# Turning six more tiles by DMA, and moving the output product of turned tiles behind the MLP block

## The chip, the core and the metric

The kernel runs on one core of a Trainium2 chip. The core has TensorE (PE in the profile; its weight loads are PEld), VectorE (DVE), ScalarE (ACT), GpSimd (POOL) and SyncE (SP), which issues nearly all DMAs. Each engine works through its own queue in the order in which the program names the instructions; they meet only in semaphores. The metric is the device time of one execution in microseconds (us), lower is better.

## What is computed

A pre-norm transformer layer on 2048 tokens of 512 channels, in float32: dilated local attention (32 heads of 16 channels, a window of 8 positions at distance 2), then an MLP of 1792 hidden channels with a squared relu.

```python
qkv = layernorm(x) @ wqkv                        # q, k, v: 32 heads x 16
idx = pos[:, None] - 2 * arange(8)[None, :]      # positions before 0 are masked
attn = softmax(einsum("bhsd,bhswd->bhsw", q, k[idx]) * 16 ** -0.5)
o = einsum("bhsw,bhswd->bhsd", attn, v[idx])
h = x + o @ wo
r = relu(layernorm(h) @ w1 + b1)
out = h + (r * r) @ w2 + b2
```

## The kernel before

**Tiles.** The 2048 tokens are 16 tiles of 128, t = 0 to 15, in four groups of four (R = 4): tiles 0 to 3 are group 0. Within a group a tile has a place i = t % 4; RI = 2 divides the places into a first and a second pair.

**Products.** Every float32 product is made of three products of numbers that are split into a high and a low part (`hi` on ACT, `lo` on DVE or POOL): high x high, and the two of high x low. That is `mm3`, 12 matmuls a block. With `lows_last` the four matmuls that need the low part of the left operand come last of the twelve. A left operand must lie turned (transposed). PE does that in four matmuls with the identity (`transposes`); the result is in PSUM, ACT casts the high part and DVE subtracts for the low part.

**Turned by DMA.** Tiles in `OV` have their attention result o, and tiles in `HV` their normalised h, turned without PE: `turn_split` (ACT, line 594) takes the float32 words apart into two planes of 16 bits, `turn_dma` (SP, line 598) turns these with a transposing DMA, and `turn_join` (ACT, line 603) puts the words together. Then follow the high part (ACT) and the low part (`lo_T`; DVE in the kernel before). Both sets are (4, 5, 8, 9, 12, 13) before: the first pair of groups 1 to 3. In this text a turned tile is one that is turned by DMA.

**Stages.** First x is normalised and multiplied with `wqkv` (`qkv`, `qkv_of`), tiles 0 to 3 by head groups and then two tiles at a time (`first_phase`, t0 = 4, 6, ... 14). The slots there are half products (6 matmuls). For group 0 a counter k runs over them: k = 0 to 11 lies in the call for t0 = 12, k = 12 to 23 in that for t0 = 14, and negative k in that for t0 = 10. The attention of the tiles runs beside it, chiefly on DVE (dots, weights, sums) and POOL (`add_up`, line 411). At set k group 0 gets its output product (`WO` = 7, 9, 13, 15 for tiles 0 to 3) and h is turned. A turning of o by PE stands at `OT`; `OK` and `HK` give the k of split, DMA and join for tiles turned by DMA.

Then come four MLP passes, u = 0 to 3, one for each group. A slot p of passes 0 to 2 holds one block of the first MLP product (`mlp1`, 12 matmuls), and one of the second (`mlp2`, 12 matmuls), which lags by LAG = 3 slots. In pass u, the next group u + 1 is prepared: its o is turned at slots `OP`, its output product is made at slots `WP` = 9, 10, 13, 14, its h is turned at 15 and 16. So tile 4 has its output product in slot 9 of pass 0 and tile 5 in slot 10.

**Order of the work.** There are two lists of chores for each slot: `due` (entered by `at`) and `late` (entered by `after`). At the end of a slot `end_slot` runs the due list, then `pump`, then the late list. `pump` puts attention operations into the queues as long as the planned DVE time `now["dve"]` is below the planned PE time `now["pe"]`; `pump(until=s)` goes on until the attention of the tile pair s is in the queues. As engines do not leave their order, a chore's place in these lists sets what it waits behind.

**Around the output product.** `wo_product` enters `h_add` (DVE adds the product to h, then the statistics of h), `h_norm`, `add_b2` and `spill` for the slots to come. For tiles in `AS` the statistics are made by ACT (`act_stats`, lines 181 to 183), for the others by DVE (`norm_stats`). In passes 0 to 2 the blocks of `mlp1` and of `wo_product` take the PSUM banks mm0 and mm1 in turn (`Turn.tile`). A bank of `mlp1` is read by `hidden` (ACT: relu, line 846), which `mlp1` enters in the due list of the next slot. In `first_phase` four banks are taken in turn.

Of the kernel before, what the change touches and what calls it, by code (L numbers as in the profile page):

```python
# [19 lines left out]
R = 4  # L20
# [8 lines left out]
NEG = -4.0e9  # L29
ROWS = 15  # L30
LAG = 3
AS = (4, 5, 8, 9, 12, 13)
OV = (4, 5, 8, 9, 12, 13)
HV = (4, 5, 8, 9, 12, 13)
SLOW = 1.01, 1.10, 1.06
DELAY = 3
WJ = 2
# [1 line left out]
OT = 4, 5, 10, 12  # L39
WO = 7, 9, 13, 15  # L40
HT = 20, 20, 21, 23
OK = (-6, -2, 4), (-5, -1, 5), (3, 6, 10), (4, 7, 12)
HK = (12, 15, 18), (14, 16, 19)
W2 = (18,)
LH = 3, 4, 10, 11
OP = 6, 7, 12, 13
# [12 lines left out]
def block_kernel(ctx, tc, x, wqkv, wo, w1, b1, w2, b2, out):  # L59
# [154 lines left out]
        for d, src in parts(tr, h_dst):  # L214
            hi(d, src)

    def lo_T(tr, h_dst, l_dst):
        for (d, src), h in zip(parts(tr, l_dst), h_dst):
            lo(nc.vector, d, src, h)
            dve(0.16 + 0.53 / len(h_dst))  # L220

    def mm3(ps, lh, ll, rh, rl, mid=None, at_=2 * KB, lows_last=False):

# [388 lines left out]
    def o_join(t):  # L612
        turn_join(("o", t))
        tr = planes.pop(("o", t))
        if t % R == RI:
            ohl = att.tile([P, 2, KB, P], F32R, name="ohl", tag="o", bufs=3)
            oT[t] = ohl[:, 0], ohl[:, 1]
        else:
            oT[t] = row("oh", (P, KB, P), F32R), row("ol", (P, KB, P), F32R)
        hi_T(tr, [oT[t][0]])  # L620
        after(0, lo_T, tr, [oT[t][0]], [oT[t][1]])

    def h_split(t):
        turn_split(("h", t), hn.pop(t))
# [33 lines left out]
    def wo_product(t, slots):  # L658
        ps = turn["mm"].tile("wo")
        oh, ol = oT.pop(t)  # L660
        mm3(ps, lambda k: oh[:, k, :], lambda k: ol[:, k, :],
            lambda k: wo_h[:, k, :], lambda k: wo_l[:, k, :], lows_last=t in OV)
        for n, (fn, a) in zip(slots, ((h_add, (t, ps)), (h_norm, (t,)), (add_b2, (t,)),
                                      (spill, (t,)))):
            (after if fn in (h_norm, spill) else at)(n + (fn is add_b2), fn, *a)

# [311 lines left out]
    def first_phase(t0):  # L980
        def chores(m):
            if t0 + 3 < 16:
                if m in (0, 2):
                    at(0, x_stats, t0 + 2 + m // 2)

                early = t0 == 12
                if m + early in (6, 7):
                    at(0, x_norm, t0 - 4 + m + early)
                if m in XT[early]:
                    x_T(t0 + 2 + XT[early].index(m))  # L990
            if t0 + 5 < 16 and m in (6, 9):
                at(0, load_x, t0 + 2 + m // 3)
            if jobs and m % 3 == 0:
                at(0, weight_job)
            k = t0 // 2 * 12 - 72 + m
            if k == 19:
                dve(HOLD)
            for t in range(R):
                if k == OT[t]:
                    at(0, load_h, t)  # L1000
                    if t not in OV:
                        o_T(t)
                if t in OV and k in OK[t]:
                    at(0, (o_split, lambda t: turn_dma(("o", t)), o_join)[OK[t].index(k)], t)
                if t in HV and k in HK[t]:
                    at(0, (h_split, lambda t: turn_dma(("h", t)),
                           lambda t: turn_join(("h", t)))[HK[t].index(k)], t)
                if k == WO[t]:
                    wo_product(t, (1, 3, 4, 6))
                    now["pe"] += 2.73  # L1010
                if k == HT[t]:
                    (at(0, h_parts, t) if t in HV else h_T(t))
            if k in W2:
                at(0, load_w2, W2.index(k))

        def half(m):
            end_slot(1.37)
            chores(m)

        for n in range(6):  # L1020
            chores(2 * n)
            qkv_of(t0 + n % 2, n // 2, lambda: half(2 * n + 1))
            end_slot(1.37)
# [41 lines left out]
    for u in range(R - 1):  # L1065
# [11 lines left out]
        for i in js:  # L1077
            t = R * (u + 1) + i
            if not end:
                a = i // 2 if u == 2 else 0  # L1080
                o0 = OP[i] - a
                if t in OV:
                    turned = [(o0, at, 0, o_split, t), (o0, after, 0, turn_dma, ("o", t)),
                              (o0 + 2, at, 0, o_join, t)]
# [26 lines left out]
        for p in range(FB + LAG):  # L1111
            more = 0.0
            if p == FB:
                run(due)
                dve(HOLD)
            if u < 2 and p == FB - 2:
                dve(HOLD)
            for fn, *a in sorted(todo.get(p, []), key=lambda x: x[0] is wo_product):
                fn(*a)
                more += 2.73 if fn is wo_product else 0.0  # L1120
            if p < FB:
                mlp1(u, fs[p])
                more += 2.73
                if first:
                    at(0, split_w2, p)
                    if p + 1 < FB:
                        load_w2(p + 1)
            q = p - LAG
            if q >= 0:
                f = fs[q]  # L1130
                mlp2(u, f, acc, js, q == 0, q == FB - 1,
                     (lambda: half(p)) if p in halves else None)
                more += 2.74
                if f < 12 and (need or first and p < FB - LAG):
                    free.append(place.pop(f))
                    if need:
                        at(1, fetch, need.pop(0))
            end_slot(more)
# [85 lines left out]
```

## Time and profile before

| | |
|---|---|
| median of 3 runs | 512.38 us (511.91 to 513.16) |
| the profiled execution | 512.31 us |
| its span in the profile | 510.5 us |
| granted TensorE clock, mean | 0.999 |
| busy: PE, DVE, ACT, POOL | 501.9, 376.7, 290.9, 351.2 us |
| instructions | 7598 |

The span is what the profiler recorded of the core; the execution's own time has some 1.8 us around it. A row of the time line has the start in us from the span's start, the length in us, the engine, the line of the code, the operation, what it writes and reads, and how many such were merged; in square brackets stands how long the engine was idle before it and what it waited for. In rows of tiles three figures parted by slashes are the lowest, median and highest length in ns. Line numbers can be those of helpers: line 232 is any `mm3`, 870 is `mlp2`, 150 any low part, 147 any high part, 205 a turning on PE, 639 `h_add`.

### The profile page before, as it was taken

What the parts mean: (1) busy time and instruction counts of PE and PEld (TensorE: products, weight loads), DVE (VectorE), ACT (ScalarE), POOL (GpSimd) and SP (SyncE); (2) the same over time, 40 slices, a digit from 0 to 9 for tenths busy, and PEclk for the clock granted to TensorE, in tenths of its full rate; (3) what the DMA queues carried; (4) which work ended last, traced back from release to release, by engine and by line L of the source; (5) the groups of instructions that cost most, each with busy time, mean ns of one, the idle gap of its engine ahead of it and who ended that gap; (6) DMA issues with size and microseconds to landing.
All of it is one profiled execution on the core that took longest, in us unless ns stands there. A gap on an engine that the chain in (4) does not pass through costs nothing. (4 is left out here: it accounts for less than half of the span.)

```text
span 510.5 us, 7598 instructions
## 1 busy us (share of the span) xinstructions
PE 501.9 (98%) x2460; PEld 424.4 (83%) x2460; DVE 376.7 (74%) x512; ACT 290.9 (57%) x552; POOL 351.2 (69%) x430
## 2 busy tenths in 40 slices
PE   7999999999999999999999999999999999999997
PEld 6999788888888888888888878888888888998986
DVE  5479899988998899788879979899963046832233
ACT  4634686767434767485364557264564737666541
POOL 4714799895786798786778768776897364685610
PEclk9999999999999999999999999999999999999999
DMA  8678998989677889666587955767672172444112
GB/s 264 180 225 203 256 295 299 271 285 274 204 225 214 276 301 272 200 199 174 182 253 217 226 166 163 202 199 249 207 152 67 52 217 84 160 142 133 62 42 83
DMA packets 100912, 100.52 MB, mean 197 GB/s; under 512 B 21000, under 2 KB 69384, under 8 KB 100872
## 3 DMA queue, kind: packets, MB, share of 16 engines
q1 hardware_dynamic: 99928, 99.52, 65.4%
q10 hardware_dynamic: 944, 0.52, 0.3%
q8 instruction: 19, 0.31, 0.3%
q14 instruction: 21, 0.17, 0.1%
HBM read 72.65 MB, written 24.25 MB: 190 GB/s over the span
## 5 line engine op out<-in xcount | busy, mean ns | idle before, releaser
L411 POOL TENSOR_TENSOR pr<-pr 128x512 f32<-128x512 f32 (+1 forms) x128 | 132.5, 1035 | 45.7 <-DVE pr L354 40.3
L232 PE MATMUL mm<-big_l,w_h 128*128 128x512 f32 x336 | 88.7, 390 | 0.0
L354 DVE TENSOR_TENSOR pr<-ex,v 128x1024 f32<-128x1024 f32 x64 | 78.2, 1222 | 12.8 <-POOL o L411 6.5
L343 DVE TENSOR_TENSOR pr<-qp,k 128x1024 f32<-128x1024 f32 x64 | 76.9, 1202 | 5.6 <-ACT qp L272 5.5
L377 DVE TENSOR_REDUCE ex<-pr 128x64 f32<-128x1024 f32 x64 | 78.4, 1226 | 1.9
L232 PEld LDWEIGHTS mm<-big_l,w_h 128*128 128x128 f32 x336 | 62.8, 188 | 13.0
L150 POOL TENSOR_TENSOR rl<-r,rh 128x512 fp32r<-128x512 f32 x42 | 56.2, 1339 | 19.6 <-ACT rh L147 16.5
L232 PE MATMUL mm<-big_h,xl 128*128 128x512 f32 (+1 forms) x208 | 56.0, 379 | 0.2 <-DVE xl L150 0.2
L232 PE MATMUL mm<-big_h,xh 128*128 128x512 f32 (+1 forms) x208 | 53.5, 378 | 0.7 <-ACT xh L147 0.7
L232 PE MATMUL mm<-big_l,xh 128*128 128x512 f32 (+1 forms) x208 | 52.8, 375 | 0.0
L870 PE MATMUL acc<-big_l,rh 128*128 128x512 f32 x190 | 52.2, 390 | 0.0
L870 PE MATMUL acc<-big_h,rh 128*128 128x512 f32 x190 | 52.1, 391 | 0.0
L501 ACT COPY y<-mm 128x512 f32<-128x512 f32 (+1 forms) x52 | 28.6, 552 | 41.2 <-PE mm L232 33.0
L870 PE MATMUL acc<-big_h,rl 128*128 128x512 f32 x190 | 51.7, 389 | 0.0
L846 ACT ACTIVATE r<-mm,b_sb 128x512 f32<-128x512 f32 x42 | 28.8, 685 | 32.4 <-PE mm L232 32.3
L232 PE MATMUL mm<-big_l,w_l 128*128 128x512 f32 x168 | 45.0, 389 | 0.0
L232 PEld LDWEIGHTS mm<-big_h,xh 128*128 128x128 f32 x208 | 37.6, 188 | 7.0 <-ACT xh L147 1.5
L232 PEld LDWEIGHTS mm<-big_l,xh 128*128 128x128 f32 x208 | 38.2, 188 | 6.1 <-POOL big_l L150 0.2
L232 PEld LDWEIGHTS mm<-big_h,xl 128*128 128x128 f32 x208 | 37.2, 188 | 5.8 <-DVE xl L150 0.6
L870 PEld LDWEIGHTS acc<-big_h,rl 128*128 128x128 f32 x190 | 35.7, 188 | 7.5
L870 PEld LDWEIGHTS acc<-big_l,rh 128*128 128x128 f32 x190 | 35.5, 188 | 7.4
L870 PEld LDWEIGHTS acc<-big_h,rh 128*128 128x128 f32 x190 | 34.9, 188 | 6.7
(160 smaller groups left out, 904.1 us busy)
## 6 DMA issues: line engine op xcount, KB each, us to landing
k<-qkv_d SPq DMA_DIRECT2D x48, 288.0 KB, 2.8
v<-qkv_d SPq DMA_DIRECT2D x48, 288.0 KB, 3.2
qkv_d<-y SPq DMA_DIRECT2D x18, 512.0 KB, 4.2
big_l<-w2l_d SPq DMA_DIRECT2D x24, 256.0 KB, 3.0
xt<-in_A_x_dram SPq DMA_DIRECT2D x16, 256.0 KB, 4.6
q<-qkv_d SPq DMA_DIRECT2D x32, 128.0 KB, 4.7
h<-in_A_x_dram SPq DMA_DIRECT2D x16, 256.0 KB, 3.9
h_d<-h SPq DMA_DIRECT2D x16, 256.0 KB, 3.2
```

Source lines behind the costliest of these rows:

```text
L150: eng.tensor_tensor(out=dst, in0=src, in1=h, op=ALU.subtract)
L232: nc.tensor.matmul(ps, l(k), r(k), start=(n == 0), stop=(n == 3 * KB - 1))
L343: nc.vector.tensor_tensor(out=pr.rearrange("p i w h d -> p i w (h d)"), in0=qps["now"][:, j % 2].unsqueeze(2).to_broadcast([P, RI, W, GC]) ...
L354: nc.vector.tensor_tensor(out=p2, in1=vwin, op=ALU.mult, in0=e1[:, :, :, j * GH:(j + 1) * GH].unsqueeze(4).to_broadcast([P, RI, W, GH, DH]))
L377: nc.vector.tensor_reduce(out=lf[:, :, :, j * GH:(j + 1) * GH], in_=pr, axis=X, op=ALU.add)
L411: nc.gpsimd.tensor_tensor(out=dst, in0=p2[:, :, :w], in1=p2[:, :, w:2 * w], op=ALU.add)
L501: nc.scalar.copy(y[:, :, t % RI * GC:(t % RI + 1) * GC], ps[:, :j * GC].rearrange("p (j c) -> p j c", j=j))
L846: nc.scalar.activation(r, ps, AF.Relu, bias=b1_sb[:, f:f + 1])
L870: nc.tensor.matmul(acc[j], l[:, j * P:(j + 1) * P], w[f], start=(first and n < len(js)), stop=(last and n >= len(terms) - len(js)))
```

## The change

It has three parts.

1. Group 0 joins: `OV` gets tiles 0 to 3, `HV` and `AS` get tiles 0 and 1. So six blocks (o of four tiles, h of two) are no longer turned by PE but by split, DMA and join. The statistics of h of tiles 0 and 1 go from DVE to ACT. The DMA no longer has a slot of its own: it is entered in the late list of the split's slot, and `OK` and `HK` have two numbers a tile, split and join. Tile 0's o is split at k = -6 and joined at k = 3, tile 1's at -5 and 4, tile 2's at 3 and 10, tile 3's at 4 and 11; h of tile 0 at 11 and 18, of tile 1 at 13 and 19.
2. In passes 0 to 2 the output product of a tile in `OV` (tiles 4, 5, 8, 9, 12, 13) is given to PE behind the slot's `mlp1` block instead of ahead of it, and `h_add` of these tiles goes from the due list of that slot to its late list.
3. The low part of a joined o tile (`lo_T` in `o_join`) is made by GpSimd instead of DVE, and is not counted in `now["dve"]`.

A shift of two slots for tiles of a second pair in `OV` is written too, but no such tile from group 1 on is in `OV`, so it does nothing here.

```diff
-AS = (4, 5, 8, 9, 12, 13)
-OV = (4, 5, 8, 9, 12, 13)
-HV = (4, 5, 8, 9, 12, 13)
+AS = (0, 1, 4, 5, 8, 9, 12, 13)
+OV = (0, 1, 2, 3, 4, 5, 8, 9, 12, 13)
+HV = (0, 1, 4, 5, 8, 9, 12, 13)
...
-OK = (-6, -2, 4), (-5, -1, 5), (3, 6, 10), (4, 7, 12)
-HK = (12, 15, 18), (14, 16, 19)
+OK = (-6, 3), (-5, 4), (3, 10), (4, 11)
+HK = (11, 18), (13, 19)
...
-    def lo_T(tr, h_dst, l_dst):
+    def lo_T(tr, h_dst, l_dst, eng=nc.vector):
         for (d, src), h in zip(parts(tr, l_dst), h_dst):
-            lo(nc.vector, d, src, h)
-            dve(0.16 + 0.53 / len(h_dst))
+            lo(eng, d, src, h)
+            if eng is nc.vector:
+                dve(0.16 + 0.53 / len(h_dst))
...
-        after(0, lo_T, tr, [oT[t][0]], [oT[t][1]])
+        after(0, lo_T, tr, [oT[t][0]], [oT[t][1]], nc.gpsimd if t in (0, 1, 2, 3, 4, 5, 8, 9, 12, 13) else nc.vector)
...
-            (after if fn in (h_norm, spill) else at)(n + (fn is add_b2), fn, *a)
+            late_ = fn in (h_norm, spill) or fn is h_add and t in OV and R <= t and t % R < RI
+            (after if late_ else at)(n + (fn is add_b2), fn, *a)
...
                 if t in OV and k in OK[t]:
-                    at(0, (o_split, lambda t: turn_dma(("o", t)), o_join)[OK[t].index(k)], t)
+                    if k == OK[t][0]:
+                        at(0, o_split, t)
+                        after(0, turn_dma, ("o", t))
+                    else:
+                        at(0, o_join, t)
...
-                o0 = OP[i] - a
+                o0 = OP[i] - a - (2 if i >= RI and t in OV else 0)
...
-            for fn, *a in sorted(todo.get(p, []), key=lambda x: x[0] is wo_product):
+            body = todo.get(p, [])
+            behind = [x for x in body if x[0] is wo_product and x[1] in OV]
+            for fn, *a in sorted(body, key=lambda x: x[0] is wo_product):
+                if [fn, *a] in behind:
+                    continue
                 fn(*a)
                 more += 2.73 if fn is wo_product else 0.0
             if p < FB:
...
+            for fn, *a in behind:
+                fn(*a)
+                more += 2.73
             q = p - LAG
```

The `HK` chores are rewritten in the same way as those of `OK`.

More of the change, by code (lines that the diff above doesn't have):

```diff
@@ L1003, in chores @@
                 if t in OV and k in OK[t]:
-                    at(0, (o_split, lambda t: turn_dma(("o", t)), o_join)[OK[t].index(k)], t)
-                if t in HV and k in HK[t]:
-                    at(0, (h_split, lambda t: turn_dma(("h", t)),
-                           lambda t: turn_join(("h", t)))[HK[t].index(k)], t)
+                    if k == OK[t][0]:
[3 more added lines that the diff above has]
+                        at(0, o_join, t)
+                if t in HV and k in HK[t]:
+                    if k == HK[t][0]:
+                        at(0, h_split, t)
+                        after(0, turn_dma, ("h", t))
+                    else:
+                        at(0, turn_join, ("h", t))
                 if k == WO[t]:
```

## The prediction

> **What bounds the kernel now.** I read the page's busy times first, then the chain of work that ended last, then the waits, and then the time line engine by engine at the three places that the change touches.
>
> ```profile
> PE 501.9 (98%) x2460; PEld 424.4 (83%) x2460; DVE 376.7 (74%) x512; ACT 290.9 (57%) x552; POOL 351.2 (69%) x430
> ```
>
> TensorE (PE) is busy for 98% of the span. So PE work that goes away is a gain, other engines' work counts only where PE waits for it, and little idle time is left to win.
>
> ```profile
> 317.01 0.44 PE tr L205 x4
> 317.45 2.75 PE mm L232 x12
> 320.19 2.72 PE acc L870 x12
> ```
>
> The chain (start, length, what) is PE block after PE block: 12 matmuls of a product take 2.72 us, so four take 0.91; turning a tile on PE takes 0.44 us, and the block behind it 0.03 more: 0.47 a tile.
>
> ```profile
> 294.18 1.07 PE L232 MATMUL wo<-wo_l,oh 128*128 128x512 f32 x4
> 295.86 1.20 PE L232 MATMUL wo<-wo_h,ol 128*128 128x512 f32 x4 [0.61 <-DVE ol L150]
> 296.89 1.08 PE L232 MATMUL mm<-big_l,w_h 128*128 128x512 f32 x4
> ```
> ```profile
> PE wo L232 <- DVE ol L150: 1.2, 2, 0.6
> ```
>
> Here PE waits for VectorE (DVE) inside the output product of tile 8. These eight matmuls should take 1.81 us and take 2.71 (294.18 to 296.89): 0.90 lost, 0.12 of it as slower matmuls after the restart. The waits (total, times, longest) show two such places, tiles 8 and 9: 1.8 us together.
>
> **What the change removes.** Six turnings on PE (o of tiles 0 to 3, h of tiles 0 and 1): 6 x 0.47 = 2.8 us, all on the path. The two waits for the low part: it now comes from GpSimd (POOL), and is wanted one MLP block (2.72 us) later, so they should go: 1.8 us. Gain: 4.6 us.
>
> **What the move behind the MLP block adds.** Look at pass 0, slot 9, where tile 4 has its output product.
>
> ```profile
> 206.83 1.07 PE L232 MATMUL mm<-big_l,w_h 128*128 128x512 f32 x4
> ```
> ```profile
> 203.65 0.68 DVE L150 TENSOR_TENSOR big_l<-raw,big_h 128x512 fp32r<-128x512 f32 x1
> 207.03 0.69 DVE L639 TENSOR_TENSOR h<-wo,h 128x512 f32<-128x512 f32 x1 [2.70 <-PE wo L232]
> 207.64 1.22 DVE L377 TENSOR_REDUCE ex<-pr 128x64 f32<-128x1024 f32 x1
> 208.77 1.22 DVE L343 TENSOR_TENSOR pr<-qp,k 128x1024 f32<-128x1024 f32 x1
> ```
> ```profile
> 207.76 0.63 ACT L181 ACTIVATE scrap<-h 128x512 f32<-128x512 f32 x1 [2.38 <-DVE h L639]
> ...
> 209.47 0.60 ACT L147 CAST big_h<-raw 128x512 fp32r<-128x512 f32 x1
> 209.98 0.68 ACT L846 ACTIVATE r<-mm,b_sb 128x512 f32<-128x512 f32 x1
> ```
>
> Before, the order on PE is product of tile 4, first MLP product of slot 9 (from 206.83), second MLP product (209.55), product of tile 5 (212.27), first MLP product of slot 10 (214.99). DVE adds the product to h from 207.03, 0.20 after the next block began; ScalarE (ACT) takes the statistics of h from 207.76 to 209.47 (1.71 us), and the relu of slot 9 follows in its queue.
>
> PSUM has two banks for these products, taken in turn. With one output product between them, the first MLP products of slots 9 and 10 have the same bank, before and after; slot 10's must wait for slot 9's relu. Before, that relu had time until 214.99. After, PE runs: first MLP product of slot 9, tile 4's product, second MLP product, and then slot 10's first MLP product at once. And the relu still stands behind the statistics of tile 4 in ACT's queue, because h_add moves into the late list of slot 9 and the relu is in the due list of slot 10. Counted from the start of the second MLP product: addition starts at 0.20, statistics 0.73 later, relu 1.71 after that, 0.68 long, some 0.05 to wake PE: 3.4 us. PE is there after 2.72. So PE stalls 0.66, plus 0.12 for the restart: 0.8 us even if DVE is early. The same holds for slot 11 behind slot 10. Six tiles (4, 5, 8, 9, 12, 13): 6 x 0.8 = 4.8 us, which alone eats the gain.
>
> That is the floor; it grows where DVE comes late to the addition. In the late list it stands behind the attention operations that the pump puts into the slot. Pass 0: DVE is free of slot 8's work at about 203.7; five or six operations at some 1.2 us bring it to 209.6 to 210.8, while the product, now from 206.83 to 209.55, lets it start at 209.75. That adds 0 to 1.0; I take 0.5. In slot 10 PE has just lost time and DVE is early. Pass 1 is worse:
>
> ```profile
> 293.69 1.22 DVE L343 TENSOR_TENSOR pr<-qp,k 128x1024 f32<-128x1024 f32 x1
> 294.82 0.97 DVE L150 TENSOR_TENSOR ol<-pl,oh 128x512 fp32r<-128x512 f32 x1
> ...
> 301.68 1.22 DVE L354 TENSOR_TENSOR pr<-ex,v 128x1024 f32<-128x1024 f32 x1 [0.39 <-POOL o L411]
> 302.94 1.23 DVE L377 TENSOR_REDUCE ex<-pr 128x64 f32<-128x1024 f32 x1
> ```
> ```profile
> 292.60 2.11 POOL L411 TENSOR_TENSOR pr<-pr 128x512 f32<-128x512 f32 x2 [1.24 <-DVE pr L354]
> 294.79 0.46 POOL L411 TENSOR_TENSOR o<-pr 128x128 f32<-128x128 f32 x1
> 295.21 1.74 POOL L150 TENSOR_TENSOR rl<-r,rh 128x512 fp32r<-128x512 f32 x1
> ```
> ```profile
> L150 POOL TENSOR_TENSOR rl<-r,rh 128x512 fp32r<-128x512 f32 x42 | 56.2, 1339 | 19.6 <-ACT rh L147 16.5
> ```
>
> Slot 9's PE work starts at 293.27 (294.18 less 0.91) and DVE is still in slot 8 until 294.8. From there the pump puts five operations before the old addition of tile 9, and by its account one more in the new order, with the addition and the low part no longer counted ahead. Run straight through, six operations end at 302.0. But 301.68 shows an operation waiting for POOL's sum of the one before. POOL is free at 295.25; the low part of tile 8, 1.34 us, now comes first, then rl, 1.3, then the sum, 2.65 (292.60 to 295.25): 300.5, and three operations behind it make 304.1. So the addition starts at 302.0 to 304.1, the relu lets PE go 3.2 us later, at 305.2 to 307.3, and PE stands there from 301.43. The stall is 3.8 to 5.9, which is 3.1 to 5.2 above the floor; I take 4.1. Pass 2 has nearly no attention left, and DVE waits long for the product:
>
> ```profile
> 395.11 0.69 DVE L639 TENSOR_TENSOR h<-wo,h 128x512 f32<-128x512 f32 x1 [6.54 <-PE wo L232]
> ```
>
> so it stays at the floor. [...]
>
> **What group 0 adds.** Each tile turned by DMA costs ACT a split, a join and a cast:
>
> ```profile
> L594 ACT COPY pl<-o x6: 1037/1040/1042, 187.2 to 372.5; 128x1024 uint16<-128x1024 uint16 x6
> ...
> L603 ACT COPY pl<-o x6: 1160/1170/1175, 198.1 to 383.8; 128x1024 uint16<-128x1024 uint16 x6
> L147 ACT CAST oh<-pl x6: 621/622/623, 199.3 to 385.0; 128x512 fp32r<-128x512 f32 x6
> L150 DVE TENSOR_TENSOR ol<-pl,oh x6: 683/812/1017, 203.0 to 387.6; 128x512 fp32r<-128x512 f32 x6
> ```
> ```profile
> 120.67 0.59 ACT L501 COPY y<-mm 128x512 f32<-128x512 f32 x1 [0.16 <-PE mm L232]
> 121.16 0.58 ACT L147 CAST oh<-tr 128x512 fp32r<-128x512 f32 x1
> 121.64 0.38 ACT L400 ACTIVATE ex<-ex 128x256 f32<-128x256 f32 x1
> 121.95 0.55 ACT L147 CAST w_h<-raw 128x448 fp32r<-128x448 f32 x1
> 122.40 0.82 ACT L200 ACTIVATE xt<-xt,rs 128x512 f32<-128x512 f32 x1
> ```
> ```profile
> 125.50 0.60 PE L205 MATMUL tr<-ident,xt 128*128 128x128 f32 x4
> ```
>
> At half-slots k=3 and k=4 stand both joins of tiles 0 and 1 and both splits of tiles 2 and 3: each half-slot gets 1.17 + 0.62 + 1.04 = 2.83 us of ACT, against 1.36 of PE. Behind them, at k=5, ACT normalises x tile 14, which PE turns at k=7. ACT is free at 120.51; 2.83, the y copy to its successor 0.49, 2.83, then ex 0.31, w_h 0.45 and xt 0.82 end at 128.2. PE, without two turnings, comes at 125.50 - 0.94 = 124.6: a stall of 3.6 us; some overlap of neighbours makes it 3.5. Low end 2.0, if ACT gets there over a microsecond early; high end 5.0: SyncE (SP) queues each transposing DMA right behind its split, so that the loads of k, q, v, x and weights behind it wait for ACT too. The splits at k=-6 and -5 I cost at nothing (ACT idles in between and has caught up by k=0), the h splits and joins of tiles 0 and 1 too (slots with ACT waiting for PE); without that cover they cost what is in the high end. ACT's new statistics of tiles 0 and 1 replace DVE's and lie behind the products.
>
> **Sum.** 512.3 (the profiled execution's own time, 0.1 below the median of the runs) - 2.8 - 1.8 + 4.8 + 0.5 + 4.1 + 3.5 = 520.6 us. With the ends of its terms: 517.6 to 524.
>
> **Rivals.** A, faster: the floor isn't there. It decides at the start of slot 10's first MLP product: if that block does not have the bank of slot 9, PE never waits for the relu, the move is pure cover, and with the joins covered too the time is 512.3 - 4.6 = 507.7. Against it: the banks alternate strictly, with one product between. For it: nothing in the trace shows a bank; 0.08. B, no change: the floor alone, DVE no longer late in pass 1 and ACT in time at k=5: 512.5. For it: DVE is spared low parts, and its waits for output products go; 0.12. C, slower by less: one of these two large terms comes and not the other, 516 to 517; 0.2. D, slower by more: PE's clock drops after the two long stalls. The start of the kernel has a row:
>
> ```profile
> 1.34 4.18 PE L918 MATMUL tr<-ident 128*128 128x128 f32 x24 [1.34 <-POOL mhalf L904]
> ```
>
> These 24 took 4.18 us, four of them 0.70, against 0.44 later. That is up to 2.0 us per cold start: 520.6 + 4 = 524.6. Against it: no stall before was long enough to show it in mid-run; 0.12. [...]
>
> **How the numbers follow.** The forecast has 0.48, A 0.08, B 0.12, C 0.2, D 0.12. A difference under 0.3% (1.5 us) can't be told from none. Faster is A, 0.08; within 0.3% is most of B, 0.11; slower is the rest, 0.81. The range leaves out A and most of B and goes up past D: 513.4 to 526.
>
> **What would show it.** In the new profile: turnings of o and h down by 24 matmuls; PE idle before the first MLP products of slots 10 and 11 in each pass, released by ACT's relu (line of `hidden`), smallest 0.7, largest in pass 1; PE idle before the turning of x tile 14 near 125, released by ACT. If PE's waits for ACT add up to less than 3 us, I am wrong, and A or B holds.

## The result, and the profile after

The changed kernel takes 537.74 us (median of 4 runs, 537.19 to 539.02) against 512.58 us for the kernel before: ratio 1.0495, 95% interval 1.0472 to 1.0518. It is slower by 25 us. The prediction was 520.6, with a range up to 526.0: the direction was right, the size was not.

The busy times on the page after, and its row of the granted TensorE clock (tenths of full speed, 40 equal slices of the span):

```profile
PE 509.2 (95%) x2436; PEld 426.7 (79%) x2436; DVE 369.1 (69%) x498; ACT 305.8 (57%) x574; POOL 362.0 (67%) x440
PEclk9999999997999999989999997999999999999999
```

The 24 matmuls of six turnings are gone (2460 to 2436), and yet PE is busy 7.3 us longer. The span grew by 26.7 us (510.5 to 537.2). So 19.4 us are more idle time of PE, and 7.3 are matmuls that ran longer, net of the turnings that are gone; the two sevens and the eight in the clock row show where.

The waits of PE after (what it waits for; total us, times, longest):

```profile
PE mm L233 <- ACT r L848: 9.8, 6, 4.3
PE tr L205 <- ACT xt L200: 7.0, 2, 6.6
PE wo L233 <- ACT ohl L147: 1.6, 1, 1.6
PE mm L233 <- ACT y L502: 1.2, 1, 1.2
PE mm L233 <- DVE big_l L150: 0.9, 2, 0.7
```

Before, the largest line behind the start of the kernel was 1.2 us, the wait for the low part. That line is gone. In its place PE waits for ACT: for the relu (line 848, `hidden`), for the normalised x, for a high part, for a copy of y.

The same waits in the time line of PE:

```profile
131.22 1.12 PE L205 MATMUL tr<-ident,xt 128*128 128x128 f32 x4 [6.56 <-ACT xt L200]
228.24 2.07 PE L233 MATMUL mm<-big_l,w_h 128*128 128x512 f32 x4 [4.27 <-ACT r L848]
324.38 2.07 PE L233 MATMUL mm<-big_l,w_h 128*128 128x512 f32 x4 [3.68 <-ACT r L848]
336.00 1.20 PE L233 MATMUL mm<-big_l,w_h 128*128 128x512 f32 x4 [0.48 <-ACT r L848]
```

They are x tile 14; slot 10 of pass 0; slots 10 and 11 of pass 1. Behind each of the three long waits four matmuls take 2.07 us instead of 1.07, or a turning 1.12 instead of 0.66. Three stretches of the table by windows, each right behind one of these waits, have the granted clock at half (the column after POOL's):

```profile
131.20:133.00 1.80, 1.78 (x7) 1.59 (x8) 1.80 (x4) 1.15 (x2) 0.51 (x1) 0.50 1.06 333
...
228.20:230.00 1.80, 1.76 (x4) 1.47 (x5) 1.71 (x4) 1.75 (x4) 1.21 (x4) 0.50 0.81 298
...
324.30:326.30 2.00, 1.92 (x5) 1.54 (x6) 1.88 (x4) 1.93 (x5) 1.32 (x3) 0.50 0.80 251
```

Following the same place of PE's work through both traces (start before, start after, in us) shows where the time goes:

| block | before | after | behind by |
|---|---|---|---|
| first phase, k = 0 | 115.01 | 114.96 | -0.1 |
| first MLP product of pass 0 | 163.29 | 173.40 | 10.1 |
| pass 0, slot 9 | 204.11 | 215.57 | 11.5 |
| pass 0, slot 11 | 220.43 | 238.58 | 18.2 |
| pass 1, slot 9 | 293.27 | 312.38 | 19.1 |
| pass 1, slot 11 | 311.40 | 336.00 | 24.6 |
| pass 3, begin | 432.20 | 459.00 | 26.8 |

Group 0 costs 10.1, the output products of pass 0 cost 6.7, those of pass 1 5.5; the other 4.5 are short waits elsewhere. In the 10.1 are: turnings -2.9, the wait for x tile 14 with its restart 6.7, slow matmuls behind it 2.1, the wait for the high part of tile 2's o 1.9, and two waits for copies of y, 0.8 and 1.6.

### The profile page after: what moved, and what is told of

Read it like the earlier page. It is cut to its first block, busy times and chain, and to the rows that moved or that the text cites. A ratio compares the mean times of both kernels' runs of the same rounds, so it can differ in the third digit from the quotient of the medians.

```text
span 537.2 us, 7582 instructions
## 1 busy us (share of the span) xinstructions
PE 509.2 (95%) x2436; PEld 426.7 (79%) x2436; DVE 369.1 (69%) x498; ACT 305.8 (57%) x574; POOL 362.0 (67%) x440
## 5 line engine op out<-in xcount | busy, mean ns | idle before, releaser
L233 PE MATMUL mm<-big_l,w_h 128*128 128x512 f32 x336 | 92.6, 402 | 12.0 <-ACT r L848 9.8
L355 DVE TENSOR_TENSOR pr<-ex,v 128x1024 f32<-128x1024 f32 x64 | 78.0, 1221 | 10.4 <-POOL o L412 5.2
L150 POOL TENSOR_TENSOR rl<-r,rh 128x512 fp32r<-128x512 f32 x42 | 54.4, 1296 | 17.9 <-ACT rh L147 16.2
L233 PE MATMUL mm<-big_l,w_l 128*128 128x512 f32 x168 | 46.4, 399 | 0.0
L502 ACT COPY y<-mm 128x512 f32<-128x512 f32 (+1 forms) x52 | 28.5, 551 | 20.9 <-PE mm L233 10.4
```

The costliest lines, as they stand in the source:

```text
L150: eng.tensor_tensor(out=dst, in0=src, in1=h, op=ALU.subtract)
L233: nc.tensor.matmul(ps, l(k), r(k), start=(n == 0), stop=(n == 3 * KB - 1))
L355: nc.vector.tensor_tensor(out=p2, in1=vwin, op=ALU.mult, in0=e1[:, :, :, j * GH:(j + 1) * GH].unsqueeze(4).to_broadcast([P, RI, W, GH, DH]))
L502: nc.scalar.copy(y[:, :, t % RI * GC:(t % RI + 1) * GC], ps[:, :j * GC].rearrange("p (j c) -> p j c", j=j))
```

## Experiments

All times are medians. The kernel before, timed along with them, took 511.94 us beside the first four kernels (labels e1 to e4), and 512.43, 511.98 and 512.33 us beside the next three groups of four. "Old sets" means that group 0 is turned by PE, as before.

**One part of the change at a time.** Old sets, all else as changed:

```diff
-AS = (0, 1, 4, 5, 8, 9, 12, 13)
-OV = (0, 1, 2, 3, 4, 5, 8, 9, 12, 13)
-HV = (0, 1, 4, 5, 8, 9, 12, 13)
+AS = (4, 5, 8, 9, 12, 13)
+OV = (4, 5, 8, 9, 12, 13)
+HV = (4, 5, 8, 9, 12, 13)
```

> The changed kernel with group 0 as before (the three sets without tiles 0 to 3); the move behind the MLP block and the low parts on GpSimd stay. Theory 1: the loss has two separate seats, group 0 (10.1 us up to the first MLP pass, 1.3 us just behind it) and the blocks of slots 9 to 11 (13.6 us net in three passes). Then this run is at 537.7 - 11.4 = 526.3 us and keeps PE's waits for ACT's relu in slots 10 and 11. Rival: the second seat is only an after-effect of the first (engines still behind from group 0); then it comes to 514 us or less.

Measured: 522.37, ratio 1.0201 (1.0177 to 1.0226). Parts 2 and 3 alone cost 10.4 us. PE waits for the relu 1.15 and 1.36 us in pass 0, 3.62 in pass 1 (with the slow clock behind it), and 0.47 at three other places. So the second seat stands by itself, as theory 1 has it, but it is 4 us smaller than expected.

Part 1 alone (low parts of group 0 on GpSimd, of the others on DVE; products and `h_add` where they were before):

```diff
-            behind = [x for x in body if x[0] is wo_product and x[1] in OV]
+            behind = []
-            late_ = fn in (h_norm, spill) or fn is h_add and t in OV and R <= t and t % R < RI
+            late_ = fn in (h_norm, spill)
```

> The kernel before with only the first part of the change: tiles 0 to 3 turned by DMA (their low parts on GpSimd, statistics of h of tiles 0 and 1 on ACT); no product moved, low parts of the other tiles on DVE. Theory 1: 512.6 + 11.4 = 524 us, with PE's wait of some 6.6 us before the turning of x tile 14 and the drop of the granted clock behind it. Together with the run that puts group 0 back the two losses add up to that of the whole change (25 us). Rival: the parts cost only together; then this one lies at 512 to 515 us.

Measured: 525.22, ratio 1.0259 (1.0233 to 1.0285), so 13.3 us for a part that was predicted to cost 0.7. The two prices add to 23.7 of the 25 us.

**The late list.** The changed kernel with `h_add` back in the due list (the second edit above alone):

> The changed kernel with h_add of tiles 4, 5, 8, 9, 12, 13 again in the due list, ahead of the pump; the product stays behind the MLP block. Theory 1: the wait for the relu stays, since statistics still stand ahead of it in ACT's queue, but comes down to its floor of 0.64 idle in all six places, and the two drops of the clock go: 537.7 - 5.2 - 5.9 = 526.6 us. Rival: GpSimd's extra low parts make DVE late, not the place of the addition; then the two long stalls of 4.3 and 3.7 us stay and the time is within 2 us of 537.7.

Measured: 546.94, ratio 1.0683 (1.0651 to 1.0714): 9 us worse than the changed kernel, not better. This expectation fell. The time lines of ACT, POOL and DVE of this kernel show what replaced the old wait:

```profile
246.14 0.81 ACT L200 ACTIVATE hn<-h,rs 128x512 f32<-128x512 f32 x1 [6.41 <-POOL rs L190]
246.86 0.67 ACT L848 ACTIVATE r<-mm,b_sb 128x512 f32<-128x512 f32 x1
```
```profile
241.05 2.11 POOL L412 TENSOR_TENSOR pr<-pr 128x512 f32<-128x512 f32 x2 [6.50 <-DVE pr L355]
...
245.91 0.19 POOL L190 TENSOR_TENSOR rs<-nm,rs 128x1 f32<-128x1 f32 x1
```
```profile
233.41 0.69 DVE L640 TENSOR_TENSOR h<-wo,h 128x512 f32<-128x512 f32 x1 [3.65 <-PE wo L233]
```

In the due list the addition waits for the later product (3.65 us) with all of the slot's attention behind it on DVE. POOL's attention sum then waits 6.50 us for DVE; the small operations that finish the statistics stand behind that sum; ACT's normalising waits 6.41 us for them; and the relu stands behind the normalising. PE waited 3.77 us there. In these rows each engine kept the order of its queue, and each stood behind an operation that waited for the next engine.

**Statistics behind the relu.** The changed kernel, with ACT's statistics of tiles 4, 5, 8, 9, 12, 13 entered one slot later, behind the relu:

```diff
-        (act_stats if t in AS else norm_stats)(t, h)
+        if t in AS and t >= R:
+            at(1, stats_norm, t)      # act_stats, then h_norm in the late list
+        else:
+            (act_stats if t in AS else norm_stats)(t, h)
```

> The changed kernel, but ACT's statistics of h of tiles 4, 5, 8, 9, 12, 13 are entered in the due list of the next slot, so that they stand behind the relu of the slot that has the product; h_norm follows them. Product behind the MLP block and late addition as in the change. Theory 1: no wait for the relu is left in slots 10 and 11 (6.7 us in pass 0, 7.4 in pass 1, 1.5 in pass 2, with the drops of the clock): 537.7 - 15.6 = 522 us. Rival: the relu is late because ACT as a whole or DVE is late; then the stalls stay in part and the gain is under 5 us.

Measured: 535.66, ratio 1.0462 (1.0435 to 1.0489), 2 us better than the changed kernel: within the rival's 5, and far from the theory's 522. In pass 0 slot 10's wait went and came back a slot later: PE waited 4.80 us at 242.82, since the normalising that waits for POOL's finish now stood ahead of the next relu (ACT idle 5.07 us there). In pass 1 the wait of 3.68 us gave way to two of 1.19 and 2.48. Moving one chore past one relu handed most of the wait to the next.

**The move and GpSimd's low parts, apart.** Part 2 alone (old sets, low parts on DVE), then part 3 alone (old sets, product and addition as before, by the two edits shown for part 1 alone); for part 2 alone:

```diff
-... nc.gpsimd if t in (0, 1, 2, 3, 4, 5, 8, 9, 12, 13) else nc.vector)
+... nc.vector)
```

> The kernel before with part 2 alone: the products of turned tiles behind the MLP block and their h_add in the late list; group 0 as before, low parts on DVE. It splits the 10.4 us that groups 1 to 3 cost when parts 2 and 3 are there together (522.4 against 511.9). Theory M (the move carries it: the relu of the next slot stands in ACT's queue behind statistics that wait for the later product): 521 to 524, with PE waiting for the relu ahead of slots 10 and 11 of each pass, once over 3 us. Theory L (GpSimd's low parts carry what goes beyond the floor, since they hold back the sums of the attention and so DVE): the floor alone, without the two waits for the low part, 512 - 1.8 + 4.6 = about 515, no wait over 1.5 us.

> The kernel before with part 3 alone: low parts of turned o tiles on GpSimd and not counted in DVE's plan; product ahead of the MLP block, group 0 as before. Theory M: the two waits for the low part (1.8 us) go, or come back as waits for GpSimd's; 510.2 to 512.5. Theory L: GpSimd's sums come later and DVE with them, 515 or more, with PE waits for the relu or for GpSimd's low part of over 1 us.

Measured: 522.41, ratio 1.0184 (1.0156 to 1.0213), and 523.44, ratio 1.0196 (1.0166 to 1.0226). Each costs as much as both together (522.37). The move alone has the waits for the relu that theory M names, 4.68 us the longest. But part 3 alone comes out as L has it, with waits for GpSimd's low part of over 1 us (and one of 1.58 us for the relu), and not within M's 512.5. So neither part is free, and it isn't DVE that is late in the second, but the low part itself. POOL's time line of part 3 alone, and PE's:

```profile
304.45 2.07 POOL L412 TENSOR_TENSOR pr<-pr 128x512 f32<-128x512 f32 x2
306.60 0.45 POOL L412 TENSOR_TENSOR o<-pr 128x128 f32<-128x128 f32 x1
307.01 1.26 POOL L150 TENSOR_TENSOR ol<-pl,oh 128x512 fp32r<-128x512 f32 x1
```
```profile
308.33 1.19 PE L233 MATMUL wo<-wo_h,ol 128*128 128x512 f32 x4 [3.43 <-POOL ol L150]
```

The low part takes 1.26 us, but stands behind attention sums of 2.6 us each. PE waits 1.20, 3.43 and 3.34 us for it in the three passes. Behind the MLP block the product needs the low part 2.72 us later, so the move covers most of what part 3 costs, and pays for that with the relu. That is why the parts do not add.

**Statistics on DVE.** Old sets, parts 2 and 3, and:

```diff
-AS = (4, 5, 8, 9, 12, 13)
+AS = ()
```

> Parts 2 and 3 (group 0 as before), but the statistics of h of tiles 4, 5, 8, 9, 12 and 13 are made by DVE instead of ACT, so that nothing that waits for the product stands in ACT's queue ahead of the relu, except the normalising of h. Theory ACT (statistics ahead of the relu are what PE waits for): the waits ahead of slots 10 and 11 (1.15, 1.36, 3.62 and three times 0.47 us, and 1.8 us of slow clock behind the long one) go nearly all, 511 to 515. Rival DVE (the late addition itself, or the normalising that waits for it, holds ACT anyway): the waits stay, 519 to 523.

Measured: 517.8, ratio 1.0093 (1.0071 to 1.0115), 4.6 us less than with the statistics on ACT. PE waits for no relu any more, as theory ACT has it. The time is 2.8 us over its upper end of 515, and what stands there is one wait for POOL's low part, 3.36 us at 391.98, with slow matmuls behind it.

So the low parts go to DVE too (the same kernel, with the edit of part 2 alone):

> Part 2 (product behind the MLP block), but both the low parts and the statistics of tiles 4, 5, 8, 9, 12, 13 on DVE; group 0 as before. With the statistics on DVE the move gave 517.8, and what was left of PE's waits there was one of 3.4 us for GpSimd's low part (with slow matmuls behind it) and one of 0.6 for the addition. Theory queue (an in-order engine is late only where an operation ahead waits for another engine; DVE's low part stands behind nothing that long): PE waits for neither, and the two waits of the kernel before are covered by the MLP block: 510.5, between 510 and 513. Rival load (DVE has 0.9 us of statistics and 0.7 to 0.8 of low part a tile too much): PE waits for the relu or DVE again, 515 or more.

Measured: 511.81 (10 runs), ratio 0.9998 (0.9988 to 1.0008): no difference from the kernel before. Its time lines of ACT and PE at slot 10 of pass 1, where the changed kernel lost most:

```profile
308.73 0.37 ACT L401 ACTIVATE ex<-ex 128x256 f32<-128x256 f32 x1 [6.54 <-DVE ex L397]
309.01 0.81 ACT L200 ACTIVATE hn<-h,rs 128x512 f32<-128x512 f32 x1
309.72 0.68 ACT L848 ACTIVATE r<-mm,b_sb 128x512 f32<-128x512 f32 x1
```
```profile
309.56 1.07 PE L872 MATMUL acc<-big_h,rl 128*128 128x512 f32 x4
310.47 1.17 PE L233 MATMUL mm<-big_l,w_h 128*128 128x512 f32 x4
```

The relu ends just before PE needs the bank. The two waits of the kernel before (1.8 us) are gone as well. What eats most of this gain is one new wait of 1.23 us at 251.46 for the normalised h of tile 7, behind a POOL sum.

**Low part ahead of the sums.** Part 3 alone again, with `lo_T` called in `o_join` itself and not entered in the late list:

```diff
-        after(0, lo_T, tr, [oT[t][0]], [oT[t][1]], nc.gpsimd if ...
+        lo_T(tr, [oT[t][0]], [oT[t][1]], nc.gpsimd if ...
```

> Part 3 alone, as in e6_pool_lows, but GpSimd's low part is entered right behind the join, ahead of the slot's attention sums, instead of in the late list behind them. With it behind them PE waited 1.2, 3.4 and 3.3 us for it ahead of the low matmuls of tiles 4, 8 and 12 (523.4 in all). Theory queue (the 1.3 us of the low part don't matter, the sums of 2.6 us each ahead of it do): the three waits go, 510.5 to 513. Rival (GpSimd waits in its queue for ACT's join, and the sums behind it come late instead): PE waits for relu or DVE, 515 or more.

Measured: 516.3, ratio 1.0078 (1.0057 to 1.0099). It is 7 us better than behind the sums, so most of the price was the queue and not the 1.3 us. But it is not the 510.5 to 513 of the theory: PE still waits 2.09 us for the low part in pass 2, and a relu late by 2.03 us in pass 1, which is the rival's wait, is followed by the slow clock.

**Finishing the statistics ahead of the sum.** The kernel with everything on DVE, with POOL's three finishing operations for the second pairs entered at once:

```diff
-    def norm_stats(key, src, delay=True):
+    def norm_stats(key, src, delay=True, now_=False):
...
-        if delay:
+        if delay and not now_:
             after(0, finish)
...
-        (act_stats if t in AS else norm_stats)(t, h)
+        norm_stats(t, h, True, t >= R and t % R >= RI)
```

> The same as e9_move_dve, but GpSimd's three small operations that finish the statistics of h of the second pair of each group (tiles 6, 7, 10, 11, 14, 15) are entered right behind DVE's statistics, ahead of the attention sum that the slot's pump gives to GpSimd. In e9_move_dve the sum (2.8 us) stands ahead of them for tile 7, ACT's normalising waits 2.9 us for GpSimd and PE 1.2 us for ACT, near 251. Theory: that wait goes, 510.5. Rival (GpSimd now waits in its queue for the product and its sums come later, so DVE's attention is late): PE waits elsewhere, 512 or more.

Measured: 520.53, ratio 1.0156 (1.0141 to 1.0172). The wait at 251 went, and worse ones came. Rows of POOL, ACT and PE:

```profile
412.77 0.23 POOL L164 TENSOR_SCALAR rs<-mv 128x1 f32<-128x1 f32 x1 [8.12 <-DVE mv L159]
```
```profile
427.13 1.05 ACT L147 CAST th<-traw 128x1024 fp32r<-128x1024 f32 x1 [10.43 <-POOL traw L766]
```
```profile
434.46 1.11 PE L702 MATMUL tr<-ident,hn 128*128 128x128 f32 x4 [5.29 <-ACT hn L200]
```

POOL now stands 8.12 and then 4.41 us until DVE has the statistics of the product, its sums of weights for pass 3 come late, ACT waits 10.43 us for them, and the normalising of h behind that holds PE 5.29 us. This is the rival's chain.

**Group 0: where the DMA is issued.** The kernel before with the new sets alone, so that each transposing DMA has a half-slot of its own. Other than in part 1 alone, the joins of tiles 0, 1 and 3 also come one half-slot later, and group 0's low parts are on DVE:

> The kernel before with nothing but the sets of part 1: group 0 is turned by DMA, but each transposing DMA is issued in a half-slot of its own, 2 to 4 after its split (o of tile 0: split at k = -6, DMA at -2, join at 4; then -5, -1, 5; 3, 6, 10; 4, 7, 12), as the kernel before would do it. Part 1 as changed, alone, gave 525.2 against 511.9, with PE waiting 7.1 us for x tile 14 near 125. Theory SP (the DMA right behind its split makes SP wait for ACT, the weight loads behind it come late, and ACT then waits for them): the wait shrinks to 3.5 us or less with no slow clock behind it, 515 to 519.5. Rival clump (joins and splits together on ACT, wherever the DMA stands): the wait stays at 6 to 7 us, 523 to 526.

Measured: 528.31, ratio 1.0308 (1.0274 to 1.0342). The wait in question shrank as theory SP has it, from 7.09 us to 2.84, though the slow clock behind it stayed. The two time lines of ACT say what the 4.25 us are: ACT waited 1.36 us for the weight load instead of 3.77, which is theory SP and 2.4 us; and only one join with its cast (1.8 us), not two, stood between that and x tile 14, which is the rival's clump. The total did not follow: it went up by 3, since lateness surfaced elsewhere:

```profile
127.33 1.12 PE L205 MATMUL tr<-ident,xt 128*128 128x128 f32 x4 [2.84 <-ACT xt L200]
148.32 2.07 PE L232 MATMUL wo<-wo_h,ohl 128*128 128x512 f32 x4 [3.44 <-ACT ohl L147]
...
318.94 2.07 PE L232 MATMUL wo<-wo_h,ol 128*128 128x512 f32 x4 [3.73 <-DVE ol L150]
404.13 1.20 PE L232 MATMUL wo<-wo_h,ol 128*128 128x512 f32 x4 [1.45 <-DVE ol L150]
```

For groups 1 to 3 the code is that of the kernel before, where the waits for a low part were 0.6 us. What the pump has put into DVE's queue by then can depend on what group 0 did.

**Group 0 on a quiet base.** The next kernels stand on the one with everything on DVE (511.81), so that group 0's price can be read cleanly. Group 0 has the sets of part 1 and its statistics of h on DVE; first with the places of the change, then spread:

```diff
-OK = (-6, 3), (-5, 4), (3, 10), (4, 11)
-HK = (11, 18), (13, 19)
+OK = (-6, -2, 4), (-5, -1, 5), (5, 7, 10), (6, 8, 12)     # split, DMA, join
+HK = (12, 15, 18), (14, 16, 19)
```

> The same as e9_move_dve, and group 0 with the places of the change itself: DMA in the late list of the split's slot, splits of tiles 2 and 3 at k = 3 and 4 beside the joins of tiles 0 and 1; statistics of h of tiles 0 and 1 on DVE, low parts on DVE. Part 1 as changed cost 13.3 us alone. Theory: the wait for x tile 14 (6.6 to 7.1 us) and the slow clock behind it (2.1) stay, the wait for the high part of tile 2's o (1.6 to 1.9) goes or shrinks since ACT no longer waits for the additions, the turnings give back 2.8: 5 to 9 us above e9_move_dve. Rival (the statistics on ACT carry most of group 0's price): less than 3 us above it.

> The same as e9_move_dve, and group 0 turned by DMA with its chores spread: transposing DMAs in half-slots of their own as the kernel before has them, splits of tiles 2 and 3 at k = 5 and 6 instead of 3 and 4, joins of tiles 0 to 3 at 4, 5, 10, 12, and the statistics of h of tiles 0 and 1 on DVE, low parts on DVE. Theory (ACT's crowd at k = 3 to 5, SP held by the DMA, and ACT held by statistics that wait for an addition are the whole price of group 0): PE waits less than 0.5 us for x tile 14, and the 2.8 us of turnings show, with at most 1.5 us of new waits: 1.3 to 2.8 us below e9_move_dve. Rival (24 more ACT operations of 1 to 1.2 us can't be hidden in a phase in which ACT already works four fifths of the time): 3 to 8 us above e9_move_dve.

Measured: 519.91, ratio 1.0156 (1.0141 to 1.0172), and 516.10, ratio 1.009 (1.0063 to 1.0116). With the places of the change group 0 costs 8.1 us, and its wait for x tile 14 is 6.64 us again; spread it costs 4.3, and that wait is 2.14 us. So the places carry 3.8 us. With the statistics on DVE the wait of 1.61 us for tile 2's high part is gone from the first of the two, as its theory has it. The rest is the rival's (the added ACT operations of over 1 us are 12, six splits and six joins, and not 24): waits of 0.83 and 1.24 us for copies of y, 0.74 and 0.52 later, where the turnings gain 2.8.

**Where the lateness of group 0 starts.** In the spread kernel ACT still waits in the first split for POOL's attention sum, and SP's store of y waits for ACT, as the time lines of ACT and SP show:

```profile
110.27 1.05 ACT L595 COPY pl<-o 128x1024 uint16<-128x1024 uint16 x1 [1.69 <-POOL o L412]
```
```profile
109.81 0.33 SPq L252 DMA_DIRECT2D k<-qkv_d  x1
113.95 0.38 SPq L484 DMA_DIRECT2D qkv_d<-y  x1
114.42 0.53 SPq L252 DMA_DIRECT2D v<-qkv_d  x1
115.04 0.56 SPq L441 DMA_DIRECT2D xt<-in_A_x_dram  x1
115.70 0.44 SPq L552 DMA_DIRECT2D raw<-in_B_w_dram  x1
```

The weight load goes out at 115.70. So the first splits were moved:

```diff
-OK = (-6, -2, 4), (-5, -1, 5), (5, 7, 10), (6, 8, 12)
+OK = (-3, 0, 4), (-2, 1, 5), (5, 7, 10), (6, 8, 12)
```

> The same as e10_group0_spread, but o of tiles 0 and 1 is split at k = -3 and -2 instead of -6 and -5 (DMA at 0 and 1, joins still at 4 and 5). At k = -6 ACT waited 1.7 us in the split for GpSimd's last attention sum, and SP's queue stood still from 109.8 to 114.0 behind a store that waits for ACT's copy of y. Theory (the early split is where the lateness starts): no such wait of ACT, weight loads on time, PE's wait of 2.1 us for x tile 14 under 0.5: 2 us less than e10_group0_spread (514). Rival (the lateness comes from the number of ACT's chores at k = 3 to 6): the wait stays within 0.5 us of 2.1, no change.

Measured: 518.21, ratio 1.0107 (1.0091 to 1.0124). The wait for x tile 14 went from 2.14 to 1.53 us, not under 0.5. The first half of the theory came: ACT waits neither for POOL in the split nor for a weight load, and that load goes out at 111.72. But the first transposing DMA now starts only at 117.45, and ACT waits for it in tile 0's join, ahead of x tile 14:

```profile
123.12 1.18 ACT L604 COPY pl<-o 128x1024 uint16<-128x1024 uint16 x1 [1.58 <-DMA o<-pl]
```

So the later split removed one wait and made another of the size that is left. The total rose by 2 (the two intervals overlap): a wait for a copy of y in front of tile 0's h grew to 2.75 us, with the slow clock behind it; ACT had waited 1.29 us there for the DMA of h.

The h tiles alone (from the spread kernel), and the o tiles alone (from the one with later splits):

```diff
-OV = (0, 1, 2, 3, 4, 5, 8, 9, 12, 13)
+OV = (4, 5, 8, 9, 12, 13)
```
```diff
-HV = (0, 1, 4, 5, 8, 9, 12, 13)
+HV = (4, 5, 8, 9, 12, 13)
```

> The same as e9_move_dve (511.8), and only h of tiles 0 and 1 turned by DMA (split at k = 12 and 14, DMA 15 and 16, join 18 and 19), o of group 0 by PE as before. Theory (the joins stand ahead of the copies of y at k = 18 and 19, while ACT waits for DMA and for the normalising): two turnings, 0.9 us, gained, and PE's waits of 0.8 and 1.2 us for y and 0.4 for the low part stay: 1 to 2 us above e9_move_dve. Rival (they come only with the o tiles, through lateness that is handed on): 0.5 to 1 us below it.

> The same as e13_late_splits without the h tiles: only o of tiles 0 to 3 turned by DMA, splits at k = -3, -2, 5, 6. Theory (both causes of lateness in group 0 gone): four turnings, 1.9 us, gained against e9_move_dve: 510 to 511. Rival (clump at k = 4 to 6): 1 to 3 us above e9_move_dve.

Measured: 518.76, ratio 1.0128 (1.0098 to 1.0158), and 516.97, ratio 1.0093 (1.0077 to 1.0109). Both expectations missed, in the same manner. In the h kernel the place itself costs one wait of 0.68 us; the rest is a wait of 3.30 us at 253 (1.23 in the base) and one of 2.02 at 395, in passes whose code did not change. In the o kernel the waits in group 0 are 1.17 and 1.20 us, and 1.28, 0.49, 1.02 and 1.89 us come in passes 0 and 1. A likely reason is that fewer turnings shift the plan of `pump`, and with it what stands ahead of what in all later slots; no run shows that by itself.

## Why the prediction was right or wrong

The forecast was 8.3 us above the kernel before; the profiled execution came out 26.7 above. With the forecast's terms put where they belong, less what is removed there, the 18.4 us between them lie, by the table of blocks, in group 0 (10.1 measured, 0.7 forecast), at slots 9 to 11 of pass 0 (6.7 against 2.1) and of pass 1 (5.5 against 3.9), and in the short waits of the rest (4.5 against 1.6).

**What is removed** was right: 24 matmuls fewer, and no wait for the low part of an o tile from group 1 on is left. The traces of the parts qualify the second: on POOL the low part alone would have been a loss of 11 us, and only the move covers it.

**The floor** was right in mechanism and size. The four undisturbed places (slot 11 of passes 0 and 1, slots 10 and 11 of pass 2) show 0.48 us of idle time each. From the two rows of slot 11 of pass 1 below, the block comes 0.63 us after the last ended (334.46 plus four matmuls, 0.91, is 335.37; it starts at 336.00), and its first matmuls take 1.20 instead of 1.07: 0.76 against the predicted 0.8.

```profile
334.46 1.07 PE L872 MATMUL acc<-big_h,rl 128*128 128x512 f32 x4
336.00 1.20 PE L233 MATMUL mm<-big_l,w_h 128*128 128x512 f32 x4 [0.48 <-ACT r L848]
```

That the statistics on ACT cause it is shown by the two kernels with the moved product and the statistics on DVE, in which no wait for a relu is left. So rival A fell at its own point: PE did wait for the relu of the block two before. B and C fell with it, since both large terms came.

**Pass 0, DVE late by 0.5** failed. PE stood 4.27 us at slot 10. The step said that DVE is free at about 203.7 and reaches the addition 0 to 1.0 us late. After, DVE's and ACT's rows are:

```profile
223.89 1.22 DVE L344 TENSOR_TENSOR pr<-qp,k 128x1024 f32<-128x1024 f32 x1 [0.57 <-POOL o L412]
225.03 0.68 DVE L640 TENSOR_TENSOR h<-wo,h 128x512 f32<-128x512 f32 x1
```
```profile
225.81 0.63 ACT L181 ACTIVATE scrap<-h 128x512 f32<-128x512 f32 x1 [2.09 <-DVE h L640]
...
227.52 0.67 ACT L848 ACTIVATE r<-mm,b_sb 128x512 f32<-128x512 f32 x1
```

PE finished tile 4's product near 221.0 (it began slot 9 at 215.57, two blocks of 2.72); the addition came at 225.03, 4 us late, behind seven pump operations and a wait for POOL. Without group 0 the same place shows 1.15 us (parts 2 and 3 alone), which is near the forecast of floor and 0.5; with the move alone it shows 0.54. So the step was right for parts 2 and 3 by themselves, and 3 us are lateness handed on from group 0, which the prediction treated as a closed account.

**Pass 1, 4.1 above the floor** was right in place and near in size, and in part wrong in the reason. The wait was 3.68 us against 4.9 predicted (0.8 + 4.1), and 3.62 without group 0. The rows of PE's last block ahead of it and of DVE's addition are:

```profile
319.63 1.07 PE L872 MATMUL acc<-big_h,rl 128*128 128x512 f32 x4
321.17 0.68 DVE L640 TENSOR_TENSOR h<-wo,h 128x512 f32<-128x512 f32 x1
```

PE ran out of work at 320.54 (319.63 plus 0.91), and the addition began 0.6 us later. The prediction's own figures for this gap were 0.6 if DVE runs straight through and 2.7 if POOL's low part holds up its sum, and it took the middle. The low end came: DVE waited only 0.38 us for POOL there, although the low part took 1.28 us, about the 1.34 assumed. With the move alone, which has no low part on POOL, the wait was longer still, 4.68. So this term does not need the low part on POOL; in the changed kernel it is DVE's own work ahead of the addition. Pass 2 stayed at the floor, as said.

**Group 0, 3.5 for x tile 14** failed most. The wait was 6.56 us, with 2.1 of slow matmuls behind it, and some 4 us of other waits came in group 0. PE reached x tile 14 when predicted (124.66), and the crowd on ACT had the predicted length: 7.7 us from the first join at 123.50 to the end of x tile 14 at 131.17. But it began 3.0 us later than the 120.51 of the prediction. "The splits at k=-6 and -5 I cost at nothing" is the step that failed. ACT waits there for POOL, and SP's queue behind it waits for ACT. ACT itself has caught up by k = 0, as the prediction says (a copy of y starts at 115.16, at 115.26 before); the weight load in SP's queue has not. ACT, SP and then SP before:

```profile
108.94 1.05 ACT L595 COPY pl<-o 128x1024 uint16<-128x1024 uint16 x1 [1.58 <-POOL o L412]
...
120.84 0.57 ACT L147 CAST w_h<-raw 128x448 fp32r<-128x448 f32 x1 [3.38 <-DMA raw<-in_B_w_dram]
```
```profile
110.01 1.37 SPq L599 DMA_TRANSPOSE o<-pl  x1
...
112.10 1.24 SPq L599 DMA_TRANSPOSE o<-pl  x1
...
115.69 0.46 SPq L552 DMA_DIRECT2D raw<-in_B_w_dram  x1
```
```profile
111.34 0.46 SPq L551 DMA_DIRECT2D raw<-in_B_w_dram  x1
```

The weight load goes out 4.4 us later than before; ACT waits 3.38 us for it and meets the crowd at k = 3 to 5 that much later. The prediction named this as the high end (5.0), which was too low as well, and still took the middle. Places of their own for the DMA, with one join fewer ahead of x tile 14, cut the wait to 2.8. Two more chores that were put at nothing cost time: the statistics of tiles 0 and 1 on ACT, behind which PE waited 1.61 us for tile 2's high part (gone with them on DVE), and the joins of h, behind which PE waited 0.60 and 1.25 us for copies of y. The joins are not the only cause of such waits: the o tiles alone had one of 1.20.

**Rival D, the slow clock,** had 0.12 and came three times. Against it stood "no stall before was long enough to show it", which says nothing about a kernel with new stalls. Behind the waits of 6.56, 4.27 and 3.68 us the granted clock is 0.50. The price, by the starts of the rows and without the restart's 0.13, was about 2.1 us behind x tile 14, 1.4 in pass 0 and 2.7 in pass 1, together 6.2, which the sum had at nothing. That waits of about 4 us, of which the sum held two, would bring it was not shown by the trace before, whose longest wait of PE behind the first 10 us is 0.61 us. D's "up to 2.0 us per cold start" was the author's estimate, and no run shows that term: the row at the start gives 1.5 (24 matmuls in 4.18 us, against 2.64 at 0.44 for four), and the granted clock reads 1.00 there (0 to 14 us of the trace before). So that row does not show what came. The wait of 3.43 us in part 3 alone was not followed by it (last section).

**What would show it** was right in place and releaser: the turnings fell by 24 matmuls, and PE waits for ACT before the first MLP products and x tile 14. Only "largest in pass 1" was not; it was pass 0.

What stays open: why the kernels with part of group 0 lose 1 to 3 us at single places of later passes. A shifted plan of the pump would fit; no run held the plan fixed while group 0 changed. Open for the same reason is how much of group 0's price could be won back.

## What to carry to other kernels

In these runs the cost of a chore was less its own length than what it waited for, and what was queued behind it: a 1.3 us subtraction on GpSimd cost up to 3.4 us behind sums, and 1.7 us of statistics on ACT up to 4.7. Before a chore is moved to another engine or another list, follow the wait through all the queues (product, DVE, POOL, ACT, PE), and keep whatever PE needs ahead of whatever waits for PE. Where a planner fills queues by a running account, price a change against everything that follows it, and when a sum holds waits of several us on PE, add the slow clock behind them: here 1.4 to 2.7 us behind each of the three long ones of the changed kernel.

## What the runs showed of the hardware

The granted clock of TensorE was down behind most of PE's long waits, but not behind all. Over all kernels of this text, four matmuls behind PE waits of 1.0 to 1.9 us in mid-kernel took 1.21 us at most, against 1.07 undisturbed. Behind three of the four waits from 2.02 to 2.14 us, and behind all from 2.48 us on but one of 3.43 us, four took 1.91 to 2.08 us (once eight took 3.62). Two rows from the time line of the h kernel, and one from part 3 alone with the low part ahead:

```profile
395.57 1.92 PE L233 MATMUL wo<-wo_h,ol 128*128 128x512 f32 x4 [2.02 <-DVE ol L150]
397.29 1.91 PE L872 MATMUL acc<-big_h,rh 128*128 128x512 f32 x4
```
```profile
391.70 1.21 PE L233 MATMUL wo<-wo_h,ol 128*128 128x512 f32 x4 [2.09 <-POOL ol L150]
```

Waits of 2.02 and 2.09 us, one with and one without: the granted clock was 0.70 from 395 to 397 us and 0.50 from 397 to 399 in the first, and 1.00 from 391.7 to 395 in the second. So the length alone does not decide; what else does, no run here shows. The price, by the starts of the rows, was some 1.4 to 3 us each time.
